# Key-value states from xᵀ·keys, with the values' weights applied afterwards, in a gated attention and GLU kernel

## The chip, the cores and the metric

The kernel runs on one core of a Trainium2 chip. The metric is device time in microseconds (us) of one execution, taken as the median of several. Times of single instructions come from one profiled execution. The engines are TensorE (PE, with weight loads shown apart as PEld), VectorE (DVE), ScalarE (ACT), GpSimd (POOL) and SyncE (SP), which here issues most of the DMAs.

## The reference

x has 2048 tokens of 576 features. The result mixes a linear attention with 32 heads of 18 and a gated GLU (576 to 4608 and back) by a sigmoid gate for each token.

```python
def _A_ref(x, wqkv, wo):
    q, k, v = ...                      # x @ wqkv, 32 heads of 18
    phi = lambda t: jnp.where(t > 0, t + 1, jnp.exp(t)) + 1e-6
    pq, pk = phi(q), phi(k)
    kv = jnp.einsum("bhsd,bhse->bhde", pk, v)
    z = jnp.einsum("bhsd->bhd", pk)
    num = jnp.einsum("bhqd,bhde->bhqe", pq, kv)
    den = jnp.einsum("bhqd,bhd->bhq", pq, z)[..., None] + 1e-6
    return (num / den).transpose(0, 2, 1, 3).reshape(B, S, D) @ wo

def _B_ref(x, w_gate, w_up, w_down):
    return (gelu(x @ w_gate) * (x @ w_up)) @ w_down

g = sigmoid((x * gate_w).sum(-1, keepdims=True))
return g * _A_ref(x, A_wqkv, A_wo) + (1 - g) * _B_ref(x, B_w_gate, B_w_up, B_w_down)
```

## The kernel before

Every matrix is kept as two parts, a rounded one (`hi`) and the rest (`lo`), and a product is three matmuls (hi hi, lo hi, hi lo) accumulated in PSUM. ACT writes `hi` by a copy, DVE or POOL subtracts to get `lo`. The order of the work on each engine is the order of the code (`manual_schedule`), and each engine runs its queue in order. SP's queue of DMA issues is in order too: an issue that waits for a buffer holds all behind it.

The 576 features of x, transposed (`xt`, tokens in the columns), lie in two halves of 288; each half is three row blocks, and a product over 576 features is 14 matmuls (`x_ops`). There are 16 tiles of 128 tokens, in four blocks of 512 (`x_next` loads a block, the pieces in `todo` split it, `do` takes pieces from `todo`).

*Stage 1, tiles 0 to 15* (L223 to L312). For each tile `proj_mm` (L163, matmul on L168) projects keys, values and the gate column together, 1154 columns in three chunks of 378, 326 and 450, into four PSUM banks in turn. `kv_post` (L175) turns keys into phi(k) (`e`, then `pkh`/`pkl`) and splits the values (`vt`). `kv_state` (L208, matmul on L219) accumulates keys by values over the tokens, with two columns of ones beside the values for the sums of keys, in `acc_a` and `acc_b` for the whole stage; it runs two tiles behind. The first two tiles go through the projection together, row block by row block, as weights arrive.

Between the tiles 2 and 8, `Early` prepares the first gate and up weights of the GLU in six parts. Each part loads 256 KB (`raw<-wgu`), ACT makes the `hi` of three blocks, POOL forms four differences (`sums`, L275), ACT makes their `hi` (both on L277), POOL the `lo`, and the results are stored to `wp_d` one tile later.

*Turn to the heads* (L339 to L453). Queries of two blocks are projected (`query`, L326, matmul on L333). Between them the states are read (`states_out`), masked to the heads, transposed on PE with an identity (`states_turn`, L378), and multiplied by the output weights (`head_out`, L406) to `KW`; `zmk` holds the sums of keys laid out by heads, which `den` (L428) uses.

*Mixing and GLU* (L456 on). The remaining queries, the normalised products (`mixed`, L524), and then the GLU stages (`product` on L690, `down` on L852, `unit` on L874), which take most of the time.

Of the kernel before, what the change touches and what calls it, by code (L numbers as in the profile page):

```python
# [11 lines left out]
OP = mybir.AluOpType  # L12
# [11 lines left out]
KVC = 1154  # L24
CA = 378
VW = 254
CW = 126 + NG * 64 + 128
# [12 lines left out]
def tile_gated_mix(ctx, tc, xt, xs, wkv, wq, wo, wgu, wdn, cst, out):  # L40
# [27 lines left out]

    class Scope:
# [6 lines left out]
        def banks(self, bufs):  # L76
            banks.append(self.stack.enter_context(
                tc.tile_pool(name="banks", bufs=bufs, space=PSUM, reuse_waits="tile")))
# [16 lines left out]
    bp = boot.pool("boot", side="right")  # L95
    kvs = Scope()
    kvs.banks(4)
    kvwp = kvs.pool("kvwp")
    kvw = [kvwp.tile([128, 5, KVC], F32R, name=f"kvw{i}") for i in range(2)]
# [35 lines left out]
    def w_raw():  # L135
        return raws.tile([128, KVC], F32, name="raw")

    KTS = [(i, kt) for i in range(2) for kt in range(3)]
    raw_of = {k: w_raw() if n < 2 else bp.tile([128, KVC], F32, name=f"raw{n}") for n, k in enumerate(KTS)}
    x0 = [x_raw(0, i) for i in range(2)]  # L140
    nc.sync.dma_start(raw_of[0, 0][:, :CA], wkv[0, 0, :, :CA])
    nc.sync.dma_start(x0[0][:, 0:1, :256], xt[0, 0, :, 0:1, :256])
    nc.sync.dma_start(raw_of[0, 0][:, CA:], wkv[0, 0, :, CA:])
    nc.sync.dma_start(x0[0][:, 1:2, :256], xt[0, 0, :, 1:2, :256])
    nc.sync.dma_start(raw_of[0, 1], wkv[0, 1])
    nc.sync.dma_start(x0[0][:, 2:3, :256], xt[0, 0, :, 2:3, :256])
    nc.sync.dma_start(raw_of[0, 2], wkv[0, 2])
    nc.sync.dma_start(x0[1][:, :, :256], xt[0, 1, :, :, :256])
    for kt in range(3):
        nc.sync.dma_start(raw_of[1, kt], wkv[1, kt])  # L150
    for i in range(2):
        nc.sync.dma_start(x0[i][:, :, 256:], xt[0, i, :, :, 256:])
    for n, (i, kt) in enumerate(KTS):
        x_split(0, i, x0[i], kt, 0, 256)
        for c, e in (((0, CA), (CA, KVC)) if n == 0 else ((0, KVC),)):
            w_part(kvw[i], kt, raw_of[i, kt], c, e)
    boot.close()
    keys = Scope()
    kp = keys.pool("kp", bufs=2, side="right")

    CH = [(0, 378), (378, 326), (704, 450)]
# [8 lines left out]
    pk, vt = {}, {}  # L170
    vbuf = [kp.tile([128, NG * VW], F32R, name=f"vt{i}", bufs=1) for i in range(2)]
    for v in vbuf:
        nc.vector.memset(f32(v).rearrange("p (g c) -> p g c", g=NG)[:, :, 0:2], 1.0)

    def kv_post(t, c, ps, part):  # L175
        if c == 0:
            pk[t] = (kp.tile([128, D], F32, name="e"), kp.tile([128, D], F32R, name="pkh"),
                     kp.tile([128, D], F32R, name="pkl"))
            vt[t] = vbuf[t % 2]
        r, ph, pl = pk[t]  # L180
        v3 = vt[t].rearrange("p (g c) -> p g c", g=NG)

        def k_part(lo, n):
            nc.scalar.activation(r[:, lo:lo + n], ps[:, :n], AF.Relu, scale=-1.0)
            if c == 1:
                nc.scalar.activation(v3[:, 0, 2:128], ps[:, 198:324], AF.Copy)
            nc.scalar.activation(r[:, lo:lo + n], r[:, lo:lo + n], AF.Exp, scale=-1.0)
            nc.vector.scalar_tensor_tensor(r[:, lo:lo + n], ps[:, :n], 0.0, r[:, lo:lo + n],
                                           op0=OP.max, op1=OP.add)

        if part == "k0":
            k_part(0, 378)
# [4 lines left out]
        elif part == "v":  # L197
            pieces = [(v3[:, 1:4, 2:128], v3[:, 1:4, 128:254], ps[:, :378].rearrange("p (g c) -> p g c", g=3)),
                      (v3[:, 4, 2:74], v3[:, 4, 74:146], ps[:, 378:450])]
            for hi, lo, src in pieces:  # L200
                nc.scalar.activation(hi, src, AF.Copy)
# [891 lines left out]
```

## Time and profile before

| | us |
|---|---|
| median of 3 runs (1555.43 to 1556.15) | 1555.69 |
| the profiled execution | 1556.57 |
| its span, first to last instruction | 1554.8 |

The profiled execution is 1.8 us longer than its span and 0.9 us longer than the median. Durations in a timeline are start and length in us, then the engine, the line, the operation, what it writes and reads, partitions by elements, and in brackets how long the engine was idle before it and what ended that. A matmul's length contains the depth of the pipeline, so the pace of matmuls is read from start to start.

| stretch of the span, us | what runs |
|---|---|
| 4.4 to 24.1 | projection of the first two tiles |
| 24.1 to 144.1 | projection of 14 tiles, states of 14 |
| 144.1 to 165.9 | queries, with the last two states between |
| 165.9 to 186.7 | transposes, heads, queries |
| from 186.7 | mixing, then the GLU |

In the second of these stretches a tile's projection and its state matmuls fill PE without a gap: in the stretch from 53.41 to 61.98 PE is busy 8.57 of 8.57 us, DVE 4.54, ACT 5.55 and POOL 3.40.

### The profile page before, as it was taken

The page shows a single profiled execution, that of the slowest core. Times are in us where ns is not written, and L with a number is a line of the kernel's source. Part 1 is how long each engine was busy: PE and PEld are TensorE (multiplying, and loading weights), DVE is VectorE, ACT ScalarE, POOL GpSimd, SP SyncE. Part 2 cuts the span into 40 slices and gives each one's busy share as a digit, 9 for nine tenths or more (in the row PEclk, how much of TensorE's full clock was granted, in tenths as well). Part 3 has the DMA queues.
Part 4 walks back from the last instruction along what each step waited for, and adds up shares of the span by engine and source line. Part 5 has one row for each costly group of instructions (what it writes and reads, how often), then busy time and mean ns, then how long its engine had stood idle before and what let it go on. Part 6 is the DMA issues. An engine that isn't in the chain of part 4 may idle for free.

```text
span 1554.8 us, 21238 instructions
## 1 busy us (share of the span) xinstructions
PE 1534.8 (99%) x8447; PEld 1356.9 (87%) x8447; DVE 991.3 (64%) x1342; ACT 548.5 (35%) x848; POOL 851.9 (55%) x693
## 2 busy tenths in 40 slices
PE   8999999999999999999999999999999999999997
PEld 8999789888888888888888888888888888888886
DVE  6443667366655555565655556777777767777778
ACT  6544554433433333333333322223232223222221
POOL 1410112276777768686656646556666555666663
PEclk9999999999999999999999999999999999999999
DMA  5611434665556565565545575433443443344333
GB/s 196 203 49 36 153 122 174 253 255 188 203 202 236 211 237 202 188 237 188 218 176 193 204 312 187 178 142 134 176 166 134 147 180 134 141 187 149 134 149 107
DMA packets 53883, 275.26 MB, mean 177 GB/s; under 512 B 4368, under 2 KB 23464, under 8 KB 43160
## 3 DMA queue, kind: packets, MB, share of 16 engines
q1 hardware_dynamic: 49464, 257.26, 44.4%
q10 hardware_dynamic: 2592, 9.31, 1.6%
q0 software_dynamic: 1728, 7.34, 1.3%
q8 instruction: 66, 1.08, 0.3%
q14 instruction: 33, 0.27, 0.1%
HBM read 172.41 MB, written 101.47 MB: 176 GB/s over the span
## 4 chain that ended last, share of the span: by engine, by line
PE 91%; DVE 5%; DMA 2%; issue 1%; ACT 1%; POOL 1%; SPq 0%; ACTq 0%; DVEq 0%; POOLq 0%
PE bank L690 50%; PE pair L852 15%; PE pair L874 12%; PE bank L168 7%; PE bank L333 3%; PE pair L524 2%; PE pair L219 1%; DVE e L727 1%; DVE sums L902 1%; DMA xc<-xs 1%; DMA wg<-wp_d 1%; POOL xo L476 1%; DVE h L733 1%; PE pair L168 0%; PE den L428 0%
## 5 line engine op out<-in xcount | busy, mean ns | idle before, releaser
L690 PE MATMUL bank<-xo,wu 128*128 128x512 f32 x1764 | 434.6, 393 | 4.9 <-DVE p L790 2.8
L690 PE MATMUL bank<-xo,wg 128*128 128x512 f32 x1764 | 433.6, 393 | 0.1
L690 PEld LDWEIGHTS bank<-xo,wg 128*128 128x128 f32 x1764 | 324.8, 188 | 64.4 <-DMA wg<-wp_d 0.5
L690 PEld LDWEIGHTS bank<-xo,wu 128*128 128x128 f32 x1764 | 322.4, 188 | 66.0 <-DVE p L790 3.6
L852 PEld LDWEIGHTS pair<-wd,h 128*128 128x128 f32 x1716 | 243.6, 189 | 13.8 <-DVE wd L67 0.7
L852 PE MATMUL pair<-wd,h 128*128 128x288 f32 x1716 | 250.6, 294 | 0.7 <-DVE wd L67 0.5
L730 ACT ACTIVATE h<-e 128x512 fp32r<-128x512 f32 x127 | 80.3, 632 | 375.4 <-DVE e L727 348.7
L859 DVE SCALAR_TENSOR_TENSOR acc<-pair,gate,acc 128x576 f32<-128x576 f32 x143 | 116.6, 816 | 131.0 <-PE pair L852 131.0
L879 DVE TENSOR_TENSOR sums<-pair,sums 128x576 f32<-128x576 f32 x224 | 167.7, 754 | 34.4 <-PE pair L874 26.7
L733 DVE TENSOR_TENSOR h<-e,h 128x512 fp32r<-128x512 f32 x127 | 124.9, 984 | 45.0 <-ACT h L730 44.9
L760 ACT ACTIVATE e<-e 128x512 f32<-128x512 f32 x108 | 68.1, 630 | 228.3 <-DVE e L816 93.5
L680 POOL TENSOR_TENSOR wdb<-draw,wdb 128x432 fp32r<-128x432 f32 x34 | 38.5, 1150 | 195.5 <-ACT wdb L678 195.5
L874 PEld LDWEIGHTS pair<-wdb,h 128*128 128x128 f32 x816 | 117.8, 189 | 9.3 <-DVE sums L879 1.7
L874 PE MATMUL pair<-wdb,h 128*128 128x288 f32 x816 | 123.0, 296 | 1.2 <-DVE sums L879 1.2
L168 PE MATMUL bank<-kvw,xo 128*128 128x378 f32 (+5 forms) x560 | 107.1, 345 | 5.5 <-ACT kvw L66 5.4
L168 PEld LDWEIGHTS bank<-kvw,xo 128*128 128x128 f32 (+1 forms) x560 | 97.5, 193 | 10.0 <-ACT kvw L66 5.9
L618 POOL TENSOR_TENSOR wu<-wuraw,wu 128x768 fp32r<-128x768 f32 x18 | 36.5, 2028 | 119.4 <-ACT wu L617 119.4
L874 PEld LDWEIGHTS pair<-wdb,hx 128*128 128x128 f32 x612 | 89.0, 189 | 6.3 <-ACT e L760 0.3
L874 PE MATMUL pair<-wdb,hx 128*128 128x288 f32 x612 | 92.9, 296 | 0.2
L765 ACT ACTIVATE p<-bank 128x512 f32<-128x512 f32 x72 | 43.1, 599 | 120.8 <-PE bank L690 120.3
L770 DVE TENSOR_TENSOR u<-bank,p 128x512 f32<-128x512 f32 x72 | 49.4, 686 | 42.4 <-PE bank L690 37.3
L727 DVE TENSOR_TENSOR e<-u,e 128x512 f32<-128x512 f32 x72 | 69.9, 971 | 2.5
(171 smaller groups left out, 2086.6 us busy)
## 6 DMA issues: line engine op xcount, KB each, us to landing
wp_d<-wg SPq DMA_DIRECT2D x17, 2240.0 KB, 6.7
wp_d<-wu SPq DMA_DIRECT2D x17, 2240.0 KB, 8.5
wg<-wp_d SPq DMA_DIRECT2D x17, 2240.0 KB, 8.6
wu<-wp_d SPq DMA_DIRECT2D x17, 2240.0 KB, 8.5
draw<-wdn SPq DMA_DIRECT2D x36, 576.0 KB, 9.3
wgraw<-wgu SPq DMA_DIRECT2D x18, 768.0 KB, 4.4
wuraw<-wgu SPq DMA_DIRECT2D x18, 768.0 KB, 4.4
xo<-xop_d SPq DMA_DIRECT2D x7, 1280.0 KB, 6.5
```

The costliest lines, as they stand in the source:

```text
L168: nc.tensor.matmul(out_t[:, :n], xa, kvw[i][:rows, r, lo:lo + n], start=(k == 0), stop=(k == 13))
L333: nc.tensor.matmul(ps[:R], qw[i][:rows, rw, GO[g]:GO[g] + R], xa, start=(k == 0), stop=(k == 13))
L690: nc.tensor.matmul(ps, w_, x_, start=start and i == 0, stop=i == 6, skip_group_check=not start)
L727: nc.vector.tensor_tensor(es[i], v, es[i], OP.mult)
L730: nc.scalar.activation(hs[i][:, 0], es[i], AF.Copy)
L733: nc.vector.tensor_tensor(hs[i][:, 1], es[i], f32(hs[i][:, 0]), OP.subtract)
L760: nc.scalar.activation(es[i], es[i], AF.Gelu_apprx_tanh)
L770: nc.vector.tensor_tensor(u2, b, p1, OP.add)
L852: nc.tensor.matmul(y[i], h[:, a, c], wd[:, (1 - i, 2 + i)[f], wl], start=(k == 0), stop=(k == 5))
L859: nc.vector.scalar_tensor_tensor(o, v, gate[:, 1, st:st + 1], o, op0=OP.mult, op1=OP.add)
L874: nc.tensor.matmul(y[:, j, :288], h[:, hl, c], wd[:, b, wl], start=(i == 0), stop=(i == 2))
L879: nc.vector.tensor_tensor(o, y[:, :, :288], o, OP.add)
```

## The change

The values are no longer projected. A second copy of x with tokens in the rows (`xn`, 128 x 576 a tile) is loaded and split by `xn_split` into `xg` (576 `hi` columns, then the `lo` of the last 64, then the `lo` of the first 512). `grams` multiplies xᵀ by phi(k), summed over the tokens: for each of five groups of 128 rows of `xg`, each operand pair is one matmul of 504 key columns and one of the 72 that are left, 14 pairs a tile. The sums stay in PSUM for the whole stage, in four banks of two `pair` tiles and in the banks `accx` and `accy`, so that the projection has two banks (`two`). Only keys and the gate column (578 columns, chunks of 288 and 290) are projected; three tiles instead of two go through the first projection together. Key sums are kept on DVE (`psum_k`).

Afterwards `grams_out` splits the sums, `states` multiplies the values' weights (`wv`) by them, which gives the states already turned, and `key_sums_mm` sums `psum_k` over the partitions by a matmul with ones. Both are placed between the queries. The transposes and the identity go.

```diff
-    CH = [(0, 378), (378, 326), (704, 450)]
+    CH = [(0, KH), (KH, KC - KH)]
...
+    def k_split(t):
+        r = r_k.pop(t)
+        ph, pl = pk[t] = [kp.tile([128, D], F32R, name=n) for n in ("pkh", "pkl")]
+        nc.scalar.activation(ph, r, AF.Copy, bias=EPS)
+        nc.vector.scalar_tensor_tensor(pl, r, EPS, f32(ph), op0=OP.add, op1=OP.subtract)
+        if t == 0:
+            nc.vector.tensor_scalar(psum_k, r, EPS, None, op0=OP.add)
         else:
+            nc.vector.scalar_tensor_tensor(psum_k, r, EPS, psum_k, op0=OP.add, op1=OP.add)
+
+    def xn_load(t):
+        xn_of[t] = xnp.tile([128, D], F32, name="xn", bufs=3)
+        nc.sync.dma_start(xn_of[t], xn[t])
+
+    def xn_split(t):
+        raw = xn_of.pop(t)
+        x = xg[t] = xnp.tile([128, 2 * D], F32R, name="xg")
+        nc.scalar.activation(x[:, :D], raw, AF.Copy)
+        nc.vector.tensor_tensor(x[:, D + 64:], raw[:, :512], f32(x[:, :512]), OP.subtract)
+        nc.vector.tensor_tensor(x[:, D:D + 64], raw[:, 512:], f32(x[:, 512:D]), OP.subtract)
+        if t + 3 < NST:
+            xn_load(t + 3)
+
+    def grams(t):
+        ph, pl = pk.pop(t)
+        x = xg.pop(t)
+        for n, kt in enumerate((0, 1, 4, 2, 3)):
+            c = slice(kt * 128, (kt + 1) * 128)
+            if kt < 4:
+                low = slice(D + 64 + kt * 128, D + 64 + (kt + 1) * 128)
+                ops = ((x[:, c], ph), (x[:, low], ph), (x[:, c], pl))
             else:
+                ops = ((x[:, c], ph), (x[:, c], pl))
+            for i, (a, p) in enumerate(ops):
+                begin, end = t == 0 and i == 0, t == NST - 1 and i == len(ops) - 1
+                nc.tensor.matmul(g_main[kt], a, p[:, :KM], start=begin, stop=end, skip_group_check=True)
+                nc.tensor.matmul(g_rest[:, kt * 72:(kt + 1) * 72], a, p[:, KM:], start=begin and n == 0, stop=end,
+                                 skip_group_check=True)
...
+    waiting = deque(range(FIRST))
+    for t in range(FIRST, NST):
+        for c in range(2):
             ps = bank()
             proj_mm(t, c, ps, range(14))
+            k_post(t, c, ps)
+            do(2 if t == FIRST else 1)
+        waiting.append(t)
+        ready = [waiting.popleft() for _ in range(1 if t == FIRST else min(2, len(waiting) - 1))]
+        for k in ready:
+            grams(k)
+        k_split(t)
+        for k in ready:
+            if k + 2 < NST:
+                xn_split(k + 2)
+        do(2 if t == FIRST else 1)
+        if 3 <= t < 10:
+            if t > 3:
+                early[-1].store()
+            if t < 9:
+                early.append(Early(t - 3))
                 early[-1].make()
...
+    def states(kt):
+        w, gm = wv_of.pop(kt), g_of.pop(kt)
+        for g in range(NG):
+            R = GR[g]
+            o = st[:R, 0, g * 126:(g + 1) * 126] if g < 4 else st[:R, 1, :R]
+            for i, (wl, gl) in enumerate(((0, 0), (0, 1), (1, 0))):
+                m = gm[:, gl, g * 126:(g + 1) * 126] if g < 4 else g_low[:, gl, kt * 72:(kt + 1) * 72]
+                nc.tensor.matmul(o, w[:, wl, GO[g]:GO[g] + R], m, start=(kt == 0 and i == 0 and g == 0),
+                                 stop=(kt == 4 and i == 2), skip_group_check=True)
...
+    split(g_low[:, 0], g_low[:, 1], g_rest)
+    grams_out(0)
+    grams_out(1)
+    sums_k = key_sums()
+    query(2, 1)
+    st = pair()
+    key_sums_mm(sums_k)
+    states(0)
+    states(1)
+    wv_make(3)
+    grams_out(2)
+    wv_load(4)
+    grams_out(3)
+    query(2, 2)
...
+    states(2)
+    states(3)
+    wv_make(4)
+    grams_out(4)
     wo_load(0)
     wo_load(1)
+    query(2, 3)
+    states(4)
     states_out()
+    query(2, 4)
```

`xg` has two buffers, so `xn_split(t + 1)` writes where `grams(t - 1)` has read. `Early` loads into buffers of its own (`er`), otherwise it is as it was; it runs in tiles 3 to 8.

On PE, the end of a tile before; `kvw` are the projection's weights, `vt` the values, `pkh` and `pkl` the keys:

```order
L219 MATMUL pair<-vt_205,pkh 126x254
L219 MATMUL pair<-vt_205,pkl 126x254
L219 MATMUL pair<-vt_205,pkh 72x146
L219 MATMUL pair<-vt_205,pkl 72x146
L168 MATMUL bank<-kvw_149,x_134 128x326 x7
L168 MATMUL bank<-kvw_150,xo 128x326 x7
```

And the same place now, in tile 6 (L189 is the projection, L240 and L241 the two matmuls of a Gram pair):

```order
L189 MATMUL bank<-kvw_155,x_134 128x290 x7
L189 MATMUL bank<-kvw_156,xo 128x290 x7
L240 MATMUL pair<-pkh,xg 128x504
L241 MATMUL bank<-pkh,xg 128x72
L240 MATMUL pair<-pkh,xg 128x504
L241 MATMUL bank<-pkh,xg 128x72
L240 MATMUL pair<-pkl,xg 128x504
L241 MATMUL bank<-pkl,xg 128x72
```

The ten state matmuls of 254 and 146 columns have become 14 such pairs.

On SP, the issues around the early parts before (`raw<-wgu` is an early part, `wp_d<-qw` its stores):

```order
L284 DMA wp_d_0_91<-qw_135 896x1x128
L269 DMA raw<-wgu 128x4x128
L284 DMA wp_d_1_92<-qw_136 896x1x128
L286 DMA wp_d_1_92<-qw_136 896x1x128
L269 DMA raw<-wgu 128x4x128
```

And now, in tiles 6 to 8 (`er<-wgu` is the early part, L215 `xn_load`, L249 the next block of x):

```order
L215 DMA xn<-xn 128x576
L328 DMA wp_d_0_91<-qw_135 896x1x128
L313 DMA er<-wgu 128x4x128
L249 DMA xr<-xt 128x1536 x2
L215 DMA xn<-xn 128x576
L328 DMA wp_d_1_92<-qw_136 896x1x128
L330 DMA wp_d_1_92<-qw_136 896x1x128
L313 DMA er<-wgu 128x4x128
```

A load of `xn` now stands ahead of each early part; it waits for the buffer that the same tile's `xn_split` frees.

On ACT, tiles 6 and 7 now (L197 and L198 are `e` of one chunk, L206 `pkh`, L221 `xn_split`, L321 the early part):

```order
L197 ACTIVATE e<-bank 128x288
L198 ACTIVATE e<-e 128x288
L197 ACTIVATE e<-bank 128x288
L198 ACTIVATE e<-e 128x288
L206 ACTIVATE pkh<-e 128x576
L221 ACTIVATE xg<-xn 128x576
L321 ACTIVATE qw_136<-er 128x384
L321 ACTIVATE qw_136<-er 128x512
L197 ACTIVATE e<-bank 128x288
L198 ACTIVATE e<-e 128x288
```

The early part stands behind `xn_split` of its tile and ahead of the next tile's first `e`, which frees the first of the two projection banks.

315 lines of the change are left out of this document (155 added, 160 removed).

## The prediction, made before the changed kernel ran

> **What bounds the kernel now.** I read the shares and the chain of work that ended last on the profile's page first, then that chain in order of time.
>
> ```profile
> PE 1534.8 (99%) x8447; PEld 1356.9 (87%) x8447; DVE 991.3 (64%) x1342; ACT 548.5 (35%) x848; POOL 851.9 (55%) x693
> PE 91%; DVE 5%; DMA 2%; issue 1%; ACT 1%; POOL 1%; SPq 0%; ACTq 0%; DVEq 0%; POOLq 0%
> ...
> 7.76 2.71 PE bank L168 x7
> ...
> 44.99 7.49 PE bank L168 x42
> 53.57 7.48 PE bank L168 x42
> 62.14 7.49 PE bank L168 x42
> ...
> 262.97 7.99 PE pair L524 x60
> ```
>
> TensorE (PE) is the bound: 99% busy, 91% of the chain. In the projections a token tile starts every 8.57 us (53.57 to 62.14), 7.48 for 42 projection matmuls and the rest for 10 state matmuls. So a change counts through what it does to PE's work, or by making PE wait. A 288-column matmul costs 7.99/60 = 0.133 us, one of the projection's (385 columns on average) 0.178; at the start the same matmuls took 2.71/7 = 0.387.
>
> What a narrow matmul costs shows at the end of a tile's state products, in the timeline of weight loads (PEld) and matmuls:
>
> ```profile
> 61.84 0.14 PEld L219 LDWEIGHTS pair<-vt,pkl 128*72 128x72 f32 x1
> 61.91 0.19 PEld L168 LDWEIGHTS bank<-kvw,x 128*128 128x128 f32 x1
> 62.02 0.19 PEld L168 LDWEIGHTS bank<-kvw,x 128*128 128x128 f32 x1
> ...
> 61.91 0.23 PE L219 MATMUL pair<-vt,pkl 128*72 128x146 f32 x1
> 61.98 0.36 PE L168 MATMUL bank<-kvw,x 128*128 128x326 f32 x1
> 62.17 0.46 PE L168 MATMUL bank<-kvw,x 128*128 128x326 f32 x2
> ```
>
> The 146-column matmul is past after 0.07 us, but the load of 128 weight columns that started with it at 61.91 lets the next load start only at 62.02: 0.11 us. The matmul after it goes on at 62.17 instead of 62.13 (0.19 us later, against 0.15 for its 326 columns). A 128-column load therefore has a rate of one per 0.11 us, and a shorter matmul cannot hide it.
>
> **The change, part by part** (profiled execution 1556.6 us, span 1554.8; the median of the runs is 0.9 lower).
>
> *Tiles.* Now a tile has 28 projection matmuls of 288 or 290 columns: 28 x 0.133 = 3.73 us. Its 14 Gram pairs (504 columns into one bank, 72 into another, both with 128 weight columns) cost 504/326 x 0.15 = 0.23 for the wide one, rounded down to 0.225 since part of the 0.15 is fixed, plus 0.11 for the load behind the 72 columns: 14 x 0.335 = 4.70. That is 8.43 against 8.57, 16 times: **-2.2**. By columns alone it would have been -16.
>
> *Turn to the heads.* Five transposes go (0.46, below) and a wait of 0.63 for `zmk`, which now is made three queries ahead.
>
> ```profile
> 165.94 0.66 PE L378 MATMUL pair<-cs,kvm 126*126 126x126 f32 x5
> 166.40 3.44 PE L333 MATMUL bank<-xo,qw 128*126 128x512 f32 x14
> ...
> 171.27 0.73 PE L428 MATMUL den<-hl,zmk 126*128 126x512 f32 x2 [0.63 <-DVE zmk L386]
> ```
>
> Four of those transposes have 126 weight columns: (0.46 - 0.03)/4 = 0.107 each, the loads again. The 75 new matmuls of `states` are of that size: 60 x 0.107 + 15 (72 columns) x 0.065 = 7.4. The 10 of `key_sums_mm` take 8 x 0.107 + 2 x 0.065 = 1.0. They stand on PE in a row with nothing beside them: **-1.1 + 8.4 = +7.3**. The Trainium skill's TensorE: Matmul & The Clock Gate, Back-to-back issue gap, gives some 81 ns for a 128-column matmul in a stream of load and matmul. By it, as an estimate, the narrow ones would come to about 8 us less; the rows say 0.107 to 0.11 and I keep those. `key_sums_mm` also waits for four splits of Gram banks and sums behind the last `grams`: half a microsecond for ACT's first copy, then four subtractions on DVE of 360 to 576 columns (0.5 + 0.7 + 0.7 + 0.76, by the DVE rows below) and the hand-overs, some 3.6 us. `query(2, 1)` covers 3.3, a query's 3.44 less its tail: **+0.4** (0 to 2).
>
> *Start.* Weights shrink from 1154 to 578 columns.
>
> ```profile
> 4.43 1.31 PE L168 MATMUL bank<-kvw,xo 128*128 128x378 f32 x3 [4.43 <-ACT kvw L66]
> 24.13 4.68 PE L168 MATMUL bank<-kvw,xo 128*128 128x378 f32 x28
> ```
>
> Two tiles' projection is over at 24.13 where 2 x 7.48 = 15.0 would do: 9.1 lost, 4.4 until data is there and the rest by slow matmuls. Three tiles (11.2 us of work) should end at E = 19, with 7.8 lost: PE is fed without the early pause, but works as slowly until some 10 to 12 us. **-1.3** (-3 to +1).
>
> *Tile 4, where the second block of 512 tokens opens.* These durations serve this part and the next:
>
> ```profile
> 45.13 0.47 ACT L184 ACTIVATE e<-bank 128x378 f32<-128x378 f32 x1
> 45.63 0.52 ACT L187 ACTIVATE e<-e 128x378 f32<-128x378 f32 x1
> ...
> 47.58 0.37 ACT L187 ACTIVATE e<-e 128x198 f32<-128x198 f32 x1
> 48.37 0.69 ACT L205 ACTIVATE pkh<-e 128x576 fp32r<-128x576 f32 x1 [0.43 <-DVE e L188]
> ...
> 46.18 0.55 DVE L188 SCALAR_TENSOR_TENSOR e<-bank,e 128x378 f32<-128x378 f32 x1 [2.78 <-ACT e L187]
> 46.70 0.69 DVE L67 TENSOR_TENSOR xo<-xr,xo 128x512 fp32r<-128x512 f32 x1
> 47.98 0.36 DVE L188 SCALAR_TENSOR_TENSOR e<-bank,e 128x198 f32<-128x198 f32 x1 [0.58 <-ACT e L187]
> 48.45 0.15 DVE L196 COPY gate<-bank 128x1 f32<-128x1 f32 x1
> 49.09 0.76 DVE L206 SCALAR_TENSOR_TENSOR pkl<-e,pkh 128x576 fp32r<-128x576 f32 x1 [0.49 <-ACT pkh L205]
> ```
>
> A tile gives DVE two `e` (0.46 at 288 columns), a gate copy, `pkl`, `psum_k` (0.76 each) and the low part of `xn` (0.69 + 0.2). With three tiles at once and six halves of the next x block (0.69 each), some 14.9 us stand in DVE's queue from E - 0.4 on. The last two halves of x wait besides behind `xn_split(2)`, which needs the buffer that `grams(0)` frees at E + 8.4. They are made at E + 14.5, and `proj(4, 0)` ends there rather than at E + 10.3: **+4.3** (2.8 with an empty queue, 6 at most).
>
> *Early gate weights.* This is the largest term. Before, `Early` issues its transfer with nothing ahead of it in SP's queue but stores that are ready:
>
> ```profile
> 56.80 0.62 SPq L269 DMA_DIRECT2D raw<-wgu  x1
> ...
> 59.66 1.39 PE L168 MATMUL bank<-kvw,xo 128*128 128x378 f32 x7
> ...
> 61.07 0.53 ACT L277 ACTIVATE qw<-raw 128x384 fp32r<-128x384 f32 x1 [1.30 <-DMA raw<-wgu]
> 63.05 0.63 ACT L277 ACTIVATE qw<-raw 128x512 fp32r<-128x512 f32 x1 [1.46 <-POOL raw L275]
> 63.59 0.47 ACT L184 ACTIVATE e<-bank 128x378 f32<-128x378 f32 x1
> ...
> 61.18 1.84 POOL L275 TENSOR_TENSOR raw<-raw 128x128 f32<-128x128 f32 x4 [5.01 <-DMA raw<-wgu]
> ```
>
> Issued at 56.80, landed at 61.07 (4.2 us); POOL's sums take 1.84, ACT stands still for both and reads a bank whose matmuls ended at 61.05 only at 63.59. Four banks hide that. Afterwards the projection has two banks, and SP reaches the issue only behind an `xn` load that waits for `xn_split`. ACT's queue becomes a ring: two `e` (1.5 for relu and exp of both), 0.5 for DVE, `pkh` and `xn` (1.3), DVE's `pkl`, `psum_k`, low `xn` until 5.0; SP 0.6 for `xn`, 0.6 or 1.2 for stores, issue; 4.2 to land; 1.9 of sums; 0.6 for the second half; then the next tile's first `e`. That is 12.8 us (13.4 with two stores, 14.2 with x halves as well), against PE's 8.43. A bank is free 1.2 us after its first `e` begins. Tiles 4 and 5 hide it, since two Gram products stand there. Tile 4 ends at E + 25.9 (14.6 + 1.9 + two Gram products of 4.7) and tile 5 at 39.0; ACT, late already, splits `xn` until 40.8, DVE and SP reach tile 5's early issue at 44.7, and it is landed at 48.9 and summed at 50.8. So by the ring the first `e` of tiles 6 to 9 come at E + 51.0, 63.8, 78.0 and 92.2, so `proj` of tiles 7 to 10 starts at 52.2, 65.0, 79.2 and 93.4, where PE is ready at 47.4, 60.7, 73.5 and 87.6: pauses of 4.8, 4.3, 5.7 and 5.8, **+20.6**. Bounds: 0, as in before, and 30 where each turn takes 2.5 more.
>
> *Clock after a pause.* No row shows a pause of 5 us in mid-run. The nearest is the start, where slow matmuls go on for some 6 us of busy time and lose 3. While ACT's ring decides, that is hidden; behind the last pause it isn't. Between 0 and 3 I take **+1.5**. The Trainium skill's TensorE: Matmul & The Clock Gate, Part 1, states that an idle window of some 3.4 us halves the clock; by it, as an estimate, this would be the full 3, and no row here shows it.
>
> Nothing else moves: queries, heads, mixing and the gated stages have the same PE work, and the `xn` loads (0.3 MB a tile) go beside a tile's PE work. Sum: -2.2 + 7.3 + 0.4 - 1.3 + 4.3 + 20.6 + 1.5 = +30.6, so 1587.2 as profiled and **1586** as a median.
>
> **Rivals.**
> - *The ring stays open*: the early transfer lands in time, for instance because ACT reaches `xn_split` sooner. For it: the same order cost nothing before. Against: SP's order, two banks. Without the 20.6 and the 1.5: **1564**.
> - *Faster*: the load of the next weights hides behind the wide matmul, so that 72 columns cost 0.045. 224 pairs lose 0.065 each, 14.6, and the 85 narrow matmuls 3.6. It makes the kernel faster only if the ring costs less than 12 of its 22, since while ACT sets the pace PE's gain is not seen; with an open ring it gives **1546**. Against it: 62.17 above, and the transposes.
> - *A longer ring*: the early transfer shares the queues with `xn`, stores and x, lands 2 to 3 us later, four times: **1597**.
>
> **How the numbers follow.** Forecast 0.75, open ring 0.09, hidden loads 0.07, longer ring 0.09. The forecast's own parts (start 2, tile 4 1.5, ring 6, clock 1.5) make it 1575 to 1596; the range takes in the longer ring and part of the way to the open one: 1570 to 1598. A measurement here tells 0.2%, 3.1 us, from no change. Faster 0.07, same 0.04, slower 0.89.
>
> **What would show it.** The pairs: a 504-column Gram matmul with its 72-column one every 0.335 us. The ring: waits of PE for DVE's `e` at tiles 7 to 10, and ACT waiting for the `er` transfer and for POOL before each. Tile 4: waits of its first projection for x halves. The narrow ones: 15 state matmuls in 1.5 us. If PE never waits in tiles 6 to 10, the forecast is wrong by 20 us; if the pairs take 0.27, by 14 more.

## The result and the profile after

| | before | after |
|---|---|---|
| median, us | 1555.92 (1555.43 to 1557.09) | 1598.68 (1597.21 to 1599.4) |
| span of the profiled execution, us | 1554.8 | 1597.3 |

The ratio is 1.0273, with a 95% interval of 1.0255 to 1.029: the changed kernel is slower by 42.8 us. The forecast of 1586 had the direction and the mechanism; the time lies 12.7 us above it and 0.7 us outside its range.

From the page of the changed kernel, its shares, the granted clock in 40 slices and the chain of work that ended last:

```profile
PE 1554.1 (97%) x8591; PEld 1370.1 (86%) x8591; DVE 995.7 (62%) x1343; ACT 551.1 (34%) x823; POOL 859.3 (54%) x698
...
PEclk8989999999999999999999999999999999999999
...
PE 85%; DVE 5%; DMA 4%; issue 2%; ACT 2%; POOL 1%; SPq 1%; ACTq 0%; DVEq 0%; POOLq 0%
```

PE's busy time has grown by 19 us and its idle time by 23. The chain has moved 6 points from PE to DMAs and other engines, and the clock is below nine tenths in the first and the third of the 40 slices, where the clock record of before, which begins at 12.8 us, shows it full until after the last matmul. What PE waited for in the first 200 us (line waited for: us in total, times, longest):

```profile
PE bank L189 <- DVE e L199: 21.2, 4, 7.4
...
PE pair L189 <- DVE e L199: 4.0, 1, 4.0
PE bank L189 <- DVE xo L68: 1.3, 1, 1.3
```

Four waits for `e` make 21.2 us. The next view, PE's timeline, has them in brackets, and the waits at the start above them:

```profile
22.83 2.06 PE L189 MATMUL pair<-kvw,xo 128*128 128x290 f32 x7 [3.96 <-DVE e L199]
24.68 5.59 PE L189 MATMUL bank<-kvw,xo 128*128 128x288 f32 x28
30.11 0.39 PE L240 MATMUL pair<-pkh,xg 128*128 128x504 f32 x1
30.34 0.20 PE L241 MATMUL bank<-pkh,xg 128*128 128x72 f32 x1
30.37 0.47 PE L240 MATMUL pair<-pkh,xg 128*128 128x504 f32 x1
30.68 0.20 PE L241 MATMUL bank<-pkh,xg 128*128 128x72 f32 x1
30.71 0.47 PE L240 MATMUL pair<-pkl,xg 128*128 128x504 f32 x1
...
80.51 2.05 PE L189 MATMUL bank<-kvw,x 128*128 128x288 f32 x7 [6.50 <-DVE e L199]
94.63 4.04 PE L189 MATMUL bank<-kvw,xo 128*128 128x288 f32 x28 [2.76 <-DVE e L199]
110.76 5.36 PE L189 MATMUL bank<-kvw,xo 128*128 128x288 f32 x28 [7.39 <-DVE e L199]
125.43 6.41 PE L189 MATMUL bank<-kvw,xo 128*128 128x288 f32 x28 [4.60 <-DVE e L199]
136.39 4.00 PE L189 MATMUL bank<-kvw,xo 128*128 128x288 f32 x28
144.93 4.00 PE L189 MATMUL bank<-kvw,xo 128*128 128x288 f32 x28
```

Tiles are counted from 0, as in the loop. The projections of tiles 7, 8, 9 and 10 start at 80.51, 94.63, 110.76 and 125.43, each after a pause; from tile 11 on a tile takes 8.55 us (136.39 to 144.93) without one. A Gram pair takes 0.343 us (30.37 to 30.71); the narrow matmul's time shows behind its start, in the wide one that follows (0.31 us to the next start, where the first of the row has 0.23). The third tile's second chunk waits 3.96 us at the start, which the forecast did not have. The pauses also draw the clock down, which the table of stretches shows (the number after the five engines is the granted clock):

```profile
75.00:90.00 15.00, 9.49 (x47) 9.11 (x47) 3.14 (x7) 3.89 (x8) 3.95 (x6) 0.66 0.41 121
...
105.00:122.00 17.00, 10.07 (x56) 9.30 (x56) 5.25 (x10) 5.87 (x12) 4.28 (x7) 0.80 0.32 89
...
136.00:150.00 14.00, 14.00 (x95) 13.23 (x94) 5.81 (x12) 5.73 (x11) 0.00 (x0) 1.00 0.35 112
```

A projection of 4.0 us takes 6.4 where the clock is at half (125.43). Single intervals of the clock record have half speed at 21.6 to 28.4, 38.7 to 42.1, 76.2 to 86.5, 106.9 to 113.8 and 124.0 to 130.8 us.

Last, the chain of work between 50 and 140 us, where the early gate weights `er` stand in it each time (start and length of the transfer), and ACT's two instructions on the third of them:

```profile
71.91 4.75 DMA er<-wgu
...
85.21 5.48 DMA er<-wgu
...
100.50 6.40 DMA er<-wgu
...
116.63 4.93 DMA er<-wgu
```

```profile
106.92 0.52 ACT L321 ACTIVATE qw<-er 128x384 fp32r<-128x384 f32 x1 [9.24 <-DMA er<-wgu]
108.81 0.63 ACT L321 ACTIVATE qw<-er 128x512 fp32r<-128x512 f32 x1 [1.37 <-POOL er L319]
```

This is the ring of the forecast. ACT stands still for the transfer and then for POOL, and only afterwards frees the bank that PE waits for. The four transfers took 4.75 to 6.40 us; the forecast had 4.2.

Where the two traces part, in us of the span at the same work:

| | before | after | later by |
|---|---|---|---|
| first `den` matmul (L428, now L492) | 171.27 | 216.67 | 45.4 |
| first `product` matmul (L690, L777) | 270.79 | 315.59 | 44.8 |
| first `unit` matmul (L874, L961) | 957.28 | 1002.45 | 45.2 |
| last matmul's end | 1549.87 | 1592.12 | 42.3 |

All of the loss arises before the heads. The last stage gave 2.9 back: PE waited there 4.9 us for DVE's `p` and `u` in the profiled execution of before and 1.4 in that of after. Other runs below, with the same code in that stage, show either number (e7 4.9, e8 and e11 1.4), so it is no effect of the change.

### The profile page after: what moved, and what is told of

It is laid out like the page before. It is cut to its first block, busy times and chain, and to the rows that moved or that the text cites. A ratio compares the mean times of both kernels' runs of the same rounds, so it can differ in the third digit from the quotient of the medians.

```text
span 1597.3 us, 21535 instructions
## 1 busy us (share of the span) xinstructions
PE 1554.1 (97%) x8591; PEld 1370.1 (86%) x8591; DVE 995.7 (62%) x1343; ACT 551.1 (34%) x823; POOL 859.3 (54%) x698
## 4 chain that ended last, share of the span: by engine, by line
PE 85%; DVE 5%; DMA 4%; issue 2%; ACT 2%; POOL 1%; SPq 1%; ACTq 0%; DVEq 0%; POOLq 0%
PE bank L777 48%; PE pair L939 14%; PE pair L961 12%; PE bank L388 3%; PE pair L240 2%; PE pair L611 2%; PE bank L189 2%; DMA er<-wgu 2%; DVE e L814 1%; DMA xc<-xs 1%; DVE h L820 1%; DMA wg<-wp_d 1%; POOL xo L562 1%; POOL er L319 0%; PE pair L432 0%
## 5 line engine op out<-in xcount | busy, mean ns | idle before, releaser
L777 PE MATMUL bank<-xo,wu 128*128 128x512 f32 x1764 | 434.4, 393 | 1.4 <-DVE p L877 1.4
L777 PE MATMUL bank<-xo,wg 128*128 128x512 f32 x1764 | 433.7, 393 | 0.4 <-DMA wg<-wp_d 0.4
L777 PEld LDWEIGHTS bank<-xo,wg 128*128 128x128 f32 x1764 | 324.8, 188 | 64.8 <-DMA wg<-wp_d 0.8
L777 PEld LDWEIGHTS bank<-xo,wu 128*128 128x128 f32 x1764 | 322.5, 188 | 62.2 <-DVE p L877 2.3
L820 DVE TENSOR_TENSOR h<-e,h 128x512 fp32r<-128x512 f32 x127 | 125.4, 988 | 45.1 <-ACT h L817 44.9
L961 PEld LDWEIGHTS pair<-wdb,h 128*128 128x128 f32 x816 | 117.8, 189 | 9.3 <-DVE sums L966 1.7
L961 PE MATMUL pair<-wdb,h 128*128 128x288 f32 x816 | 122.9, 296 | 1.2 <-DVE sums L966 1.2
L705 POOL TENSOR_TENSOR wu<-wuraw,wu 128x768 fp32r<-128x768 f32 x18 | 36.5, 2029 | 119.5 <-ACT wu L704 119.5
L961 PEld LDWEIGHTS pair<-wdb,hx 128*128 128x128 f32 x612 | 89.0, 189 | 6.3 <-ACT e L847 0.3
L961 PE MATMUL pair<-wdb,hx 128*128 128x288 f32 x612 | 92.9, 296 | 0.2
L189 PE MATMUL bank<-kvw,xo 128*128 128x288 f32 (+3 forms) x364 | 64.1, 335 | 21.1 <-DVE e L199 14.7
L189 PEld LDWEIGHTS bank<-kvw,xo 128*128 128x128 f32 (+1 forms) x364 | 59.7, 223 | 23.3 <-DVE e L199 15.4
```

The lines of the kernel that those rows point to most:

```text
L189: nc.tensor.matmul(out_t[:, :n], xa, kvw[i][:rows, r, lo:lo + n], start=(k == 0), stop=(k == 13))
L777: nc.tensor.matmul(ps, w_, x_, start=start and i == 0, stop=i == 6, skip_group_check=not start)
L820: nc.vector.tensor_tensor(hs[i][:, 1], es[i], f32(hs[i][:, 0]), OP.subtract)
L961: nc.tensor.matmul(y[:, j, :288], h[:, hl, c], wd[:, b, wl], start=(i == 0), stop=(i == 2))
```

## The experiments

e1, e2, e3 and e9 are edits of the changed kernel alone; e4 joins e1 and e3, e5 goes on from e4, e6 to e8 from e5, e10 from e8, and e11 and e12 each from the one before. Ratios are to the kernel before, timed on the same chip.

### e1: the early transfers issued at the head of a tile

```diff
     for t in range(FIRST, NST):
+        if t < 9:
+            early.append(Early(t - 3))
         for c in range(2):
...
-                early[-1].store()
+                early[t - 4].store()
             if t < 9:
-                early.append(Early(t - 3))
-                early[-1].make()
+                early[t - 3].make()
```

> Early part k is issued at the start of its tile, ahead of that tile's xn loads in SP's queue; nothing else moves. Theory (the transfer behind the xn load closes a ring through ACT): the four waits of PE before tiles 7 to 10 (6.5, 2.8, 7.4, 4.6 us) go, tiles 6 to 10, which took 15.2, 14.1, 16.1, 14.7 and 11.0, take 8.55 each, the clock stays at full there: 28 us less, about 1570.5. Rival (two projection banks are too few for ACT's load whatever the transfer does): at least half of the waits stay, 1584 or more.

Measured: 1576.58 us, ratio 1.0135 (1.0117 to 1.0153); 22.1 less than the changed kernel by the medians, 21.5 by the ratios, and 6 more than expected. Tiles 6 to 10 took 8.56, 8.54, 10.06, 8.56 and 8.55 us, in all 44.3 instead of 71.1, and PE's waits between 50 and 150 us came down to one:

```profile
PE bank L189 <- DVE gate L201: 1.3, 1, 1.3
```

The ring is thus what held those tiles, and 26.8 us of the loss. 6.7 of that did not reach the span (1577.2 against 1597.3). 1.2 went at the start, 1.8 in tile 4 and 3.2 in the states, where PE's timeline has this:

```profile
167.10 1.06 PE L444 MATMUL pair<-ones,wos 128*126 128x2 f32 x9 [0.33 <-DVE wos L68]
168.03 1.58 PE L433 MATMUL pair<-gt,wv 128*126 128x126 f32 x12
...
169.72 2.79 PE L433 MATMUL pair<-gt,wv 128*126 128x126 f32 x12
```

The second group of twelve takes 2.79 us and the first 1.58: the clock went to half from 169.3 to 176.2, although PE had been busy 3.07 of the 3.40 us before. This is one execution: the four of e1 took 1573.1 to 1579.0 us at mean clocks of 0.997 to 0.991, and the profiled one is the slowest of them.

### e2: `xn` split after the keys of all three first tiles

```diff
         if t:
             k_split(t - 1)
-            xn_split(t - 1)
+    for t in range(FIRST - 1):
+        xn_split(t)
     k_split(FIRST - 1)
```

> The first two xn_split stand behind the third tile's e on ACT and DVE. Theory (ACT waits for the first xn load ahead of the e of tile 2, and PE waits for that e because both chunks of tile 2 share a pair tile): the wait of 3.96 us before the second chunk falls to about 1.3, the time of relu, exp and max behind the first chunk; with less slow clock in tile 3 this is 2.7 to 6 us less, 1593 to 1596. Rival (xn is not what holds ACT): within 1 us of 1598.7.

Measured: 1598.31 us, ratio 1.0276 (1.0252 to 1.03), the same as the changed kernel. A miss: the wait at the start was still 3.3 us (3.96 in the changed kernel). ACT's timeline names another holder:

```profile
21.31 0.41 ACT L197 ACTIVATE e<-pair 128x288 f32<-128x288 f32 x1 [1.28 <-DVE psum_k L209]
```

`e` has two buffers, and the third tile's needs the one that DVE's `psum_k` of the first tile frees.

### e3: a pair of banks for each chunk of the third tile

```diff
-        both = pair() if t == 2 else None
...
-            ps_of[t, c] = ... else both[:, c]
+            ps_of[t, c] = ... else pair()[:, 0]
```

> The third tile's two chunks get a pair tile each. Theory (the shared tile makes the second chunk's matmuls wait for the first chunk's e): no wait at all before the second chunk, 4 us less, and 1 to 3.5 more where the clock does not drop to half behind it: 1591 to 1595. Rival (ACT is late anyway, so PE waits as long a little later, before tile 3 or its Gram product): 1597 to 1599.

Measured: 1593.84 us, ratio 1.0252 (1.023 to 1.0274). The interval overlaps that of the changed kernel, so the trace is the firmer evidence. PE's timeline of e3:

```profile
18.42 2.04 PE L189 MATMUL pair<-kvw,xo 128*128 128x288 f32 x14
20.30 3.93 PE L189 MATMUL bank<-kvw,xo 128*128 128x288 f32 x28
```

No wait stands between the chunks, the three tiles are done at 20.30 instead of 24.68, and the next tile's projection takes 3.93 us instead of 5.59, since the clock is full. So the start's wait came from two chunks in one `pair` tile: the second is not written while the first is still to be read. Tile 4 gave 1.5 of it back (18.66 us instead of 17.12), waiting for halves of x.

### e4: e1 and e3 together

> The early transfer ahead and the pair tiles apart, together. If the two causes are separate their gains add: 28 + 5 to 7, 1563 to 1566, with waits of PE left at tile 4's x halves (1.5) and before the key sums (0.3). If the kernel were still over 1575, something else paces stage 1.

Measured: 1574.15 us, ratio 1.0121 (1.0102 to 1.014), only 2.4 less than e1, which is within the noise; 1563 to 1566 was expected, a miss. Tile 4 took 22.56 us. With the start earlier, its x halves are what is late; PE waited 3.8 us for one. DVE's and POOL's timelines there:

```profile
30.32 0.69 DVE L68 TENSOR_TENSOR xo<-xr,xo 128x512 fp32r<-128x512 f32 x1
...
34.05 1.50 DVE L68 TENSOR_TENSOR xo<-xr,xo 128x512 fp32r<-128x512 f32 x1
```

```profile
30.52 3.52 POOL L318 TENSOR_TENSOR er<-er 128x128 f32<-128x128 f32 x4 [30.08 <-DMA er<-wgu]
34.01 2.67 POOL L322 TENSOR_TENSOR qw<-er,qw 128x384 fp32r<-128x384 f32 x2
```

POOL makes the first early part in these two rows. Beside the second (`lo`, L322), DVE's subtraction takes 1.50 us instead of 0.69. POOL's four differences take 3.52 instead of the 1.84 of later parts, beside DVE's work of that time. Whether one causes the other these rows alone don't show; e11 below bears on it. The clock was at half from 35.4 to 42.2, and again in the states (165.1 to 171.9).

### e5: the x halves three at a time in tile 3

```diff
-            do(2 if t == FIRST else 1)
+            do(3 if t == FIRST else 1)
```

> On top of e4: the six halves of the second x block are all made within tile 3's two chunks, ahead of pkh, psum_k and xn_split of that tile. Theory (tile 4 waits because these halves stand in DVE's and ACT's queues behind work that itself waits for the first Gram product): tile 4, 22.6 us in e4 against 13.1 of PE work, takes 13.1 to 15, and the clock stays up: 8 us less, about 1566. Rival (the x block lands too late, or DVE is slowed by POOL whatever the order): tile 4 still over 18.

Measured: 1569.8 us, ratio 1.0089 (1.007 to 1.0108). Tile 4 took 17.11 us, between what theory and rival gave it, the states were at full clock, and tile 8 waited 1.4 us (10.2 instead of 8.55). e5 has no ring, no wait between the chunks and 1.3 us of waits in tile 4, and is still some 14 us slower than the kernel before. Most of that is TensorE's own work in the turn to the heads: from the first query to the first `den` matmul e5 takes 37.55 us (146.21 to 183.76) and before 27.13 (144.14 to 171.27), and a Gram product that follows the first query in place of two tiles' state products is only 2.6 of that difference. The tiles without a wait take 8.55 us, no less than before's 8.57; e6 to e8 look at why.

### e6: 152 narrow columns instead of 72

From e5. The narrow matmul of a pair takes the last 152 key columns, not the last 72. The narrow matmuls of neighbouring groups then add into each other's columns, so this kernel leaves out the sums of the last key columns as such.

```diff
-                nc.tensor.matmul(g_rest[:, kt * 72:(kt + 1) * 72], a, p[:, KM:], ...
+                nc.tensor.matmul(acc[1][:, kt * 72:kt * 72 + 152], a, p[:, D - 152:], ...
```

> e5 with the 72-column matmul of each Gram pair made 152 columns wide (it takes in 80 columns that the wide one has too, so the states' last columns are overwritten with other sums). Theory (the 128-column weight load behind it sets its time, 0.11 us): nothing changes, a tile in the steady part stays at 8.55 us. Rival (columns set the time): 80 columns more are 0.033 us in each of 14 pairs, 9.0 us a tile, 7 us in all.

Measured: 1567.32 us, ratio 1.0077 (1.0062 to 1.0092). A tile took 8.51 us, 0.04 less than with 72 columns. Eighty more columns in 14 matmuls cost nothing, so columns do not set a narrow matmul's time. That the load of its weight columns does, and not a fixed cost of each matmul, shows beside the kernel before: there 146 columns with 72 weight columns took 0.07 us (61.91 to 61.98), here 152 with 128 weight columns take 0.11.

### e7: no narrow matmuls from tile 4 on

From e5; the 72 columns of the sums are left out there.

> e5 with the 72-column matmuls left out from tile 4 on (the sums of the last four heads' keys then lack those tiles). Theory (loads): a pair falls from 0.343 us to the 0.227 of a 504-column matmul, a tile from 8.55 to 6.93, 12 tiles 19.5 less. Rival (columns): 0.045 a pair, 0.63 a tile, 7.6 in all.

Measured: 1554.14 us (1550.65 to 1556.96), ratio 0.9991. Tiles without a wait took 6.92 to 6.93 us, so 14 narrow matmuls are worth 1.62 us a tile, 0.116 each, of which the shorter wide ones (0.227 us in place of 0.23) are a part. Over 12 tiles that is 19.5, and 15.7 were measured. The shorter tiles ran into loads: PE waited for `gate` in two of them, 4.4 us together, and 0.9 for `e`.

### e8: the rest turned

From e5, with the same sums in another cut. The wide matmuls take 448 key columns. The last 128 become the weights, with x's 576 columns as the moving side, so that 14 narrow matmuls become three of 512 and three of 64 columns. Five transposes with an identity turn that piece afterwards.

```diff
-KM = 504
+KM = 448
...
-                nc.tensor.matmul(g_rest[:, kt * 72:(kt + 1) * 72], a, p[:, KM:], ...
+        for i, (p, v) in enumerate(((ph, 0), (ph, 1), (pl, 0))):
+            m = (x[:, :512], x[:, D + 64:])[v], (x[:, 512:D], x[:, D:D + 64])[v]
+            nc.tensor.matmul(g_rest, p[:, KM:], m[0], ...)
+            nc.tensor.matmul(g_last, p[:, KM:], m[1], ...)
```

> e5 with the Gram product cut anew, the same result computed: 448 key columns the old way (14 matmuls a tile), and the other 128 keys as weights against all of x's columns: three pairs of 512 and 64 columns a tile, turned once at the end by five transposes. Theory (a narrow matmul costs the weight load behind it): a tile has 14 x 0.20 + 3 x (0.23 + 0.11) = 3.8 us of Gram work in place of 4.80, 7.6 in all in place of 8.55, 16 us less than e5 over 16 tiles, 1 back for the transposes: 1551 to 1556, level with the kernel before (1555) or just below. Rival (ACT and DVE set the pace once PE has 7.6 us a tile, as the waits of e7 in four tiles hint): 1558 to 1563.

Measured: 1556.7 us (1554.29 to 1559.12), ratio 1.0018 (1.0009 to 1.0027), 0.7 above the expected range. The end of a tile's sums in PE's timeline:

```profile
118.79 0.47 PE L244 MATMUL bank<-xg,pkh 128*128 128x512 f32 x1
119.10 0.19 PE L245 MATMUL bank<-xg,pkh 128*128 128x64 f32 x1
119.13 0.47 PE L244 MATMUL bank<-xg,pkl 128*128 128x512 f32 x1
```

A wide and a narrow one take 0.34 us together (118.79 to 119.13), three times a tile instead of 14. Tiles took 7.63 to 7.65 us. Tile 4, with two Gram products, took 15.3 instead of 17.1. Tile 8 did not gain (11.67, with 2.3 us of waiting and half clock from 74.8 to 78.3).

### e9: idle time filled with matmuls

The changed kernel with 40 matmuls of 128 columns, whose sums nothing reads, behind the sums of tiles 6 to 9.

```diff
+        if 6 <= t < 10:
+            for _ in range(40):
+                nc.tensor.matmul(acc[1][:, 360:488], kvw[0][:, 0, :128], kvw[0][:, 0, :128], ...)
```

> The changed kernel with 40 idle matmuls (128 columns, into columns that nothing reads, 4.4 us at full clock) behind the Gram product of tiles 6 to 9, where PE then waits anyway. Theory (ACT's ring sets the tiles' times there, and half clock costs only behind the last pause): tiles 6 to 9 stay within 0.7 us of 15.2, 14.1, 16.1 and 14.7, the clock stays at full, tile 10 falls from 11.0 to 8.55: 2 to 3 us less, 1596. Rival (half clock is paid for in each of them): 6 us less or more. If the idle matmuls don't hold the clock, nothing changes.

Measured: 1597.62 us, ratio 1.0281 (1.0267 to 1.0295), the same time as without the 160 matmuls (1598.68). They took 4.5 us a tile from start to start, 18 in all, and cost nothing in a stretch where PE waited 21. Tiles 6 to 10 took 15.29, 15.74, 13.02, 13.38 and 8.58 us; a miss for tiles 7, 8 and 9, which were expected near 14.1, 16.1 and 14.7. Nor did the clock stay at full: it was at half from 79.8 to 86.6, in tile 7. The transfers stand in the chain of e9 too:

```profile
71.66 5.10 DMA er<-wgu
...
85.32 4.12 DMA er<-wgu
...
99.26 4.96 DMA er<-wgu
...
113.96 4.92 DMA er<-wgu
```

| issue to issue, us | after | less the transfer | e9 | less the transfer |
|---|---|---|---|---|
| first to second | 13.30 | 8.55 | 13.66 | 8.56 |
| second to third | 15.29 | 9.81 | 13.94 | 9.82 |
| third to fourth | 16.13 | 9.73 | 14.70 | 9.74 |

A turn of the ring is its transfer plus a time that is the same within 0.01 us in both kernels. The third turn tells the clock's part: TensorE was at half from 106.9 to 113.8 in after and at full throughout in e9, and the rest of the turn is 9.73 and 9.74. In the first turn both kernels had a stretch at half, in the second both ran at full but for its first 1.3 us. So in the one turn that compares them the clock does not lengthen the ring, and in all three the transfer does, one for one. What tiles 6 to 10 saved together (5.1 us) was mostly lost again in the states, whose clock was at half from 189.0 to 195.9: the span is 1.8 us shorter.

### e10, e11, e12: taking away the waits of the turned version

e8 is 0.2% from the kernel before, with waits left. e10 takes the halves of x's last block three steps later; e11 also makes and stores the early parts a tile later; e12 also takes the parts of the queries' weights at the end of a tile. What the first two expectations call tile 7 is tile 8 here.

```diff
         elif t == 6:
+            todo.extend([lambda: None] * 3)
             x_next(3)
```

```diff
-        if 3 <= t < 10:
+        if 4 <= t < 11:
...
-                early[t - 3].make()
+                early[t - 4].make()
```

```diff
+            todo.extend([lambda: None] * 2)
             q_load(0, t - 10)
             q_load(1, t - 10)
+            last, first = todo.pop(), todo.pop()
+            todo.append(lambda a=first, b=last: (a(), b()))
```

> The turned rest again, with the halves of x's last block taken three steps later. In e8 tile 7's second chunk waited 2.3 us for gate, ACT stood 5.1 us at the half xo<-xr of that block before (its load had not landed, 'DMA xr<-xt'), and the clock was at half from 74.8 to 78.3, which cost about 1.7 us more; tile 7 took 11.7 us instead of 7.65. Theory (with shorter tiles a DMA is what is late, and ACT's and DVE's order carries it to TensorE): the wait and the half clock go, tile 7 is 7.65, and the time is 4.0 us under e8's, about 1552.7, which would be some 1.3 us under the kernel before. Rival (the load only moves the wait to the next instruction that needs it): tile 8 or 9 waits for the same half instead and the time stays within 1 us of e8's. Second rival: the split falls beside GpSimd's work on the early products and DVE is late for the next tile, -1 to -3 us.

> e10 with each early piece made and stored one tile later (tile 4 to 9 instead of 3 to 8; loads where they were). In e8 tile 4's projection took 7.8 us instead of 4.0: waits of 0.18 and 0.62 us for DVE, and half clock from 30.5 to 33.9, while GpSimd made the first piece (29.7 to 36.4) and DVE's instructions beside it took 0.8 to 1.5 us instead of 0.22 to 0.69. Theory (contention of DVE with GpSimd delays tile 4 and the idle time before draws the clock down): DVE in tile 4 is back at 0.69 us per half, the waits there and with them the half clock go, and the time is 2 to 3.5 us under e10's, about 1549.5 to 1550.5. Rival (the half clock comes from the idle time before 27 us, of loads and start, and not from tile 4's waits): the waits of 0.8 us go, the half clock stays, -1 us. Second rival: the backlog moves to tile 5, where GpSimd then works, and nothing is gained (within 0.7 us of e10).

> e11 with each pair of the queries' weight parts taken at the end of a tile, after that tile's keys, rather than behind a chunk's keys. (Tiles are counted from 0 here, as in the loop; what the two expectations before this one call tile 7 is tile 8 so counted.) In e11 tiles 8 to 12 ran without a wait, but tile 12's first chunk was followed on ACT by qw<-raw, whose load had been issued only at 106.9 (SP stood behind xn<-xn, 106.5): ACT stood 6.0 us, the second chunk's keys came 5 us late, tile 13 waited 2.1 us for gate and ran at half clock from 115.0 to 118.4: 11.55 us instead of 7.64. Theory (that wait was of the same kind as the one taken out of tile 8, a load carried to TensorE by ACT's order; it was only uncovered): with the parts at the end of the tile the load has a whole tile's time, no tile from 6 to 15 waits, and the time is 3.8 us under e11's, about 1551, some 0.2 per cent under the kernel before. Rival (another load comes last in its place: the values' weights in tiles 13 to 15, or the parts make the first query wait): within 1.5 us of e11's, no gain over the kernel before.

| | us | ratio to before, 95% | tile 8 | tile 13 | tile 4 |
|---|---|---|---|---|---|
| e8 | 1556.7 | 1.0018 (1.0009 to 1.0027) | 11.67 | 7.64 | 15.29 |
| e10 | 1554.34 | 1.0 (0.9989 to 1.001) | 9.67 | 7.64 | 14.49 |
| e11 | 1554.91 | 0.9995 (0.9986 to 1.0004) | 7.64 | 11.55 | 15.98 |
| e12 | 1551.17 | 0.9978 (0.9969 to 0.9988) | 7.64 | 7.63 | 14.47 |

e10 was expected 1.3 us under the kernel before, which its interval just includes, but with tile 8 at 7.65; e11 was expected at 1549.5 to 1550.5, a miss; e12 met its 1551. In e10 the half clock of tile 8 went, and a wait of 1.9 us took the other's place: ACT now stood 5 us for an `er` transfer instead. In e11 that is gone too, but tile 13 waited. ACT's timeline of e11:

```profile
111.49 0.68 ACT L67 ACTIVATE qw<-raw 128x576 fp32r<-128x576 f32 x1 [5.97 <-DMA raw<-wq]
```

Its aim, DVE beside POOL in tile 4, was missed: POOL's differences need only the transfer and started when it had landed (30.89), however late the rest of the part is made; DVE's second x half and the waits of tile 4 stayed as they were. But the second half of POOL's work (L325) did move, from 33.91 in e10 to 46.30, and the same subtraction on DVE was beside it in e10 and without it in e11. DVE's timeline of e10, then of e11:

```profile
34.48 1.50 DVE L222 TENSOR_TENSOR xg<-xn,xg 128x512 fp32r<-128x512 f32 x1
```

```profile
34.86 0.68 DVE L222 TENSOR_TENSOR xg<-xn,xg 128x512 fp32r<-128x512 f32 x1
```

So POOL's work does slow DVE's. That tile 4 was shorter by 1.5 us in e10 and e12 than in e11 is the clock: PE waited 1.3, 1.6 and 1.6 us there in e10, e11 and e12, and half clock followed in e11 alone (33.1 to 36.5). In e12 no tile from 6 to 15 waits, and the longest waits of the first 200 us, in the start and tile 4, are:

```profile
PE bank L189 <- ACT kvw L67: 4.8, 2, 4.1
PE bank L189 <- DVE kvw L133: 1.0, 1, 1.0
PE bank L189 <- DVE xo L68: 0.8, 2, 0.6
```

So e12 is faster than both kernels, by 0.22% (0.12 to 0.31) than the one before and by some 46 us than the changed one. Its queries begin at 130.68 us instead of 144.14. The states take back most of these 13.5: `den` starts at 167.35 instead of 171.27.

## Why the prediction was 12.7 us short

**Direction and bound: right.** PE is still the bound, and the change counted through PE's work and waits. Waits for `e` before tiles 7 to 10, ACT behind the `er` transfer and POOL before each, and a pair of matmuls limited by its weight load are all there.

**Tiles: -2.2 forecast, -0.4 measured.** A pair takes 0.343 us, not 0.335. The wide matmul was rounded down to 0.225 and is 0.23 (30.11 to 30.34), and the narrow one is 0.11. e6 and e7 show the other part as it was told: 152 columns cost what 72 cost, and without the narrow ones a tile is 1.62 us shorter. So hidden loads, the rival that was faster, are out. (Its condition was mis-summed: 30.6 without the 22.1 of ring and clock and without the 18.2 it saves leaves -9.7, so the ring would have had to cost less than 10 us, not 12.)

**Turn to the heads: +7.3 and +0.4 forecast, right within a microsecond.** The changed kernel takes 37.55 us from the first query to the first `den` matmul (179.12 to 216.67), 10.4 more than before, of which 2.6 is the last Gram product: 7.8. PE's timeline of the changed kernel:

```profile
190.54 0.24 PE L443 MATMUL pair<-ones,wos 128*126 128x2 f32 x1
191.11 1.06 PE L443 MATMUL pair<-ones,wos 128*126 128x2 f32 x9 [0.33 <-DVE wos L68]
192.03 1.52 PE L432 MATMUL pair<-gt,wv 128*126 128x126 f32 x12
193.38 0.33 PE L432 MATMUL pair<-g_low,wv 128*72 128x72 f32 x3
193.55 1.51 PE L432 MATMUL pair<-gt,wv 128*126 128x126 f32 x12
194.90 0.33 PE L432 MATMUL pair<-g_low,wv 128*72 128x72 f32 x3
195.06 3.48 PE L388 MATMUL bank<-xo,qw 128*126 128x512 f32 x14
```

Fifteen state matmuls take 1.52 us (192.03 to 193.55; forecast 1.5), key sums and two states 4.5, and the wait is 0.33. The Trainium skill's TensorE: Matmul & The Clock Gate, LDWEIGHTS, gives the time of a load as its columns divided by 1.2, in ns: 107 for 128 columns, 105 for 126, 60 for 72. The rows agree within 8 ns: (193.38 - 192.03)/12 = 0.112 for 126 columns and (193.55 - 193.38)/3 = 0.057 for 72.

**Start: the step that failed.** The prediction said three tiles' projection ends at E = 19 us, -1.3. It ended at 24.68, 5.7 later, the largest single part of the miss. "PE is fed without the early pause" overlooked that the third tile's two chunks share one `pair` tile, and that its `e` waits for a buffer: a wait of 3.96 us, and half clock behind it. e3 took the shared tile away and E was 20.3, so this is 4.4 of the 5.7.

**Tile 4: the number right, in part by luck.** 17.1 us against 13.35 in tile 5, with the same matmuls: +3.8, where +4.3 was forecast. But only 1.5 of it is waiting for x halves; most of the rest is half clock (38.7 to 42.1), which this term did not have.

**Early ring: the mechanism right, one term of it too small.** The forecast counted 12.8, 14.2 and 14.2 us for a turn, 8.6, 10.0 and 10.0 of them beside the transfer. Measured are 13.30, 15.29 and 16.13, and 8.55, 9.81 and 9.73 beside the transfer. So the part worked out from rows held within 0.3 us, and the transfer was mis-sized: 4.2 us forecast, 4.75 to 6.40 measured. The rival *a longer ring* had named it, with shared queues as the cause. Why the transfers are longer no run shows, and two rows speak against that cause alone: before, the transfer issued at 65.87 took 4.0 us with a load of x issued right behind it and the DMA engines busy throughout, and in the last 2.0 us of the longest transfer here (104.9 to 106.9) they were busy for 7% and moved 22 GB/s. The four transfers together are 4.8 us longer than forecast, which is some 4 of the 12.7 us; that this rival's 1597 lies so near the measured time is otherwise chance.

**Clock: +1.5 forecast, nearly four times that measured.** The prediction had half clock cost time only behind the last pause. e9 supports that for the ring in the one turn that compares the two clocks. Behind the last pause it cost 2.4 (tile 10, 10.96 us against 8.55). What it cost in tiles 3 and 4, 1.7 us each, had no term of its own.

The sum, at the first `den` matmul: 30.6 forecast; start +5.7; tile 7's projection at E + 55.8 instead of 52.2, of which 1.7 is tile 3's half clock and 0.6 the transfer before it, with 1.3 not followed up, +3.6; the three turns to tile 10's, 44.9 instead of 41.2, +3.7; tile 10 +1.0 (2.4 for the clock instead of 1.5, and 0.1 of pace); pace of tiles 11 to 15, +0.6. That is 45.2, and 45.4 was measured. The end of the span had 2.9 less from the last stage.

What stays open: why the transfers were longer; why the clock fell to half in the states in the profiled executions of e1, e4, e7 and e9 and not in those of the changed kernel, e2, e3, e5 and e6, with the same matmuls there, and whether it does so in every execution of a kernel; and how much of tile 4 is due to POOL's differences beside DVE, since no run took those away.

## What to carry to other kernels

Before counting columns, look at which of a pair of instructions sets the pace: a narrow matmul costs its weight load, so cut the operands such that few matmuls are narrow (e8 got 0.9 us a tile by turning one piece), and count what a cheaper tile then has to wait for. A transfer that an in-order engine waits for belongs ahead of every issue that itself waits for that engine; once behind it, transfer, engine and buffer form a ring whose length replaces the bound, and e1 undid some 21 us with three moved lines. Where an expected gain does not come, take the waits away one at a time and look for the next: e10 and e11 each removed a wait and found another load behind it, and the time only fell below the kernel before with the last (e12).

## What the runs showed of the hardware that was not expected

- Half clock also followed waits shorter than the clock's step. The clock changed in steps of about 3.4 us (half for 3.4, 6.8 or 10.2). In e8 half clock for 3.4 us came behind a wait of 2.26 us, with PE busy for 1.15 of the 3.41 us before it (71.46 to 74.87); in e10 a wait of 1.9 was not followed by it, and short waits of 1.6 in all in tile 4 were in e11 and not in e12. The Trainium skill's TensorE: Matmul & The Clock Gate, Part 1, has the clock halved after an idle window of some 3.4 us that runs freely. The steps agree; e8 shows that half clock can come without a whole idle window.
- The clock also fell where PE counted as busy: after 3.07 us busy of 3.40 in e1, with matmuls of 2 and 126 columns in that stretch, at a cost of about 3 us. No run shows that the few columns are the cause.
- DVE's subtraction of 512 columns took 1.50 us beside POOL's, and 0.68 when POOL's work was moved away (e10, e11); POOL's four differences took 3.52 us beside DVE's work (e4) and 1.84 where DVE stood idle. Both are longer.
- 160 matmuls, 18 us of PE's time, left the time as it was (e9).
